# Casting the output by column halves, storing it from two engines, and a shorter last piece of the output projection

## The chip, the cores and the metric

One core of a Trainium2 chip. The metric is the device time of one execution, in microseconds (us). The median before the change is 525.68 us over the first 3 runs. The device time is some 2 us longer than the span of the trace, which runs from the first to the last instruction; positions below are in the span. In the views of the profile, PE is TensorE (the matrix products), DVE is VectorE, ACT is ScalarE and SP is SyncE; a q behind a name marks that engine's instruction queue, where stores are issued. The granted clock is the share of full speed that the chip allowed TensorE.

## The reference, cut to what matters

```
xn  = layernorm(x)                                   # x: [4, 1, 640]
out = x + attention(xn, k_cache, v_cache, wq, wo)    # 32 heads of 192, the last 2048 positions of the caches
        + (silu(xn @ w1) * (xn @ w3)) @ w2           # w1, w3: [640, 1536], w2: [1536, 640]
```

The last step of the attention is a product with wo ([6144, 640]). Its sum over the heads, the feed-forward part and x are added in one tile of PSUM (the memory that matrix products are summed in), which is cast to bf16 and stored: 4 rows of 640 values, 5 KB.

## The kernel before

Only the end of the program matters here. The sum `acc` is one tile of PSUM. This text and the recorded ones call the place of such a tile a bank, and the records call its two groups of rows, partitions 0 to 3 and 32 to 35, quadrants. `acc` holds columns 0 to 319 of the output on partitions 0 to 3, columns 320 to 639 on partitions 32 to 35. Every row of wo is so two matmuls. The last group of heads takes wo in three pieces, loaded last in the stream.

```python
CT, B, N0, RPP = 32, 4, 320, 12
acc = ps_acc.tile([P, N0], FP32, name="acc")
nc.vector.memset(acc[:], 0.0)
...
def acc_half(i, lhsT, rhs, first=False, last=False):
    nc.tensor.matmul(acc[i * CT:i * CT + B, :], lhsT=lhsT, rhs=rhs[:, i * N0:(i + 1) * N0], start=first, stop=last)
...
def ge_proj(hg, i0, i1, last=False):          # two matmuls for each row i of wo
    oT, wo_t = oTs[hg], wos[hg]
    for i in range(i0, i1):
        acc_add(oT[:, i, 0:B], wo_t[:, i * D:(i + 1) * D], last=last and i == RPP - 1)
...
WOC = [0, RPP - 5, RPP - 2, RPP]              # pieces of 7, 3 and 2 rows a partition
for h in range(H - 2, H):
    add(NU - 6, 0, load_v, h)
add(NU - 6, 0, w2_load)
for i0, i1 in zip(WOC, WOC[1:]):
    add(NU - 6, 0, wo_load, NG - 1, i0, i1)
    add(e, 6, ge_proj, NG - 1, i0, i1, True)
add(e - 1, 8, ffn_out)
...
res = ppool.tile([B, 2, N0], BF16, tag="pr", name="res")
nc.scalar.copy(out=res[:, 1, :], in_=acc[CT:CT + B, :])
nc.vector.tensor_copy(out=res[:, 0, :], in_=acc[0:B, :])
nc.scalar.dma_start(out=out.rearrange("b s d -> (b s) d"), in_=res[:].rearrange("b i n -> b (i n)"))
```

Of the kernel before, what the change touches and what calls it, by code (L numbers as in the profile page):

```python
# [11 lines left out]
BF16 = mybir.dt.bfloat16  # L12
# [52 lines left out]
def kernel(  # L65
# [20 lines left out]
    nc = tc.nc  # L86
    P = 128
    B, Sq, D = A_x.shape
# [13 lines left out]
    CT = 32  # L102
    HB = HG * CT // P
    QW = HG * Dh
    RPP = QW // P
    RW = Dh // RPP
    NU = H * GQ
    N0 = D // 2
# [17 lines left out]
    ppool = ctx.enter_context(tc.tile_pool(name="pr", bufs=PBUFS))  # L126
# [36 lines left out]
    for k0 in range(0, KC, 2):  # L163
        n = min(2, KC - k0)
        wt = vpool.tile([P, 2, H * Dh], BF16, tag="vt")
        nc.sync.dma_start(out=wt[:, 0:n, :].rearrange("p k n -> p (k n)"),
                          in_=wq_v[:, k0:k0 + n, :].rearrange("p k n -> p (k n)"))
# [26 lines left out]
    acc = ps_acc.tile([P, N0], FP32, name="acc")  # L194
# [39 lines left out]
    for i in range(2):  # L234
# [4 lines left out]
                          in_=xn[:, LB:LB + LS * LP].rearrange("b (i e s) -> b s e i", e=LE, s=LS))  # L239
# [246 lines left out]
    def add(slot, phase, fn, *args):  # L486
        sched[slot].append((phase, len(sched[slot]), fn, args))
# [45 lines left out]
    add(17, 6, x_add, 1)  # L533


    WOC = [0, RPP - 5, RPP - 2, RPP]
    for h in range(H - 2, H):
        add(NU - 6, 0, load_v, h)
    add(NU - 6, 0, w2_load)
    for i0, i1 in zip(WOC, WOC[1:]):  # L540
        add(NU - 6, 0, wo_load, NG - 1, i0, i1)
# [4 lines left out]
        for phase, _, fn, args in sorted(sched[s], key=lambda e: (e[0], e[1])):  # L546
            fn(*args)

    res = ppool.tile([B, 2, N0], BF16, tag="pr", name="res")
    nc.scalar.copy(out=res[:, 1, :], in_=acc[CT:CT + B, :])  # L550
    nc.vector.tensor_copy(out=res[:, 0, :], in_=acc[0:B, :])
    nc.scalar.dma_start(out=out.rearrange("b s d -> (b s) d"), in_=res[:].rearrange("b i n -> b (i n)"))


# [28 lines left out]
```

## Time and profile before

| | before |
|---|---|
| device time, median of the first 3 runs | 525.68 us (525.5 to 525.7) |
| span of the profiled run | 523.48 us |
| bytes read | 222.96 MB, 426 GB/s over the span |
| last completion of a piece of wo | 520.415 us |
| from there to the end of the program | 3.064 us |

The last row is what the change can reach. I call it **the tail**: from the moment when the last piece of wo is complete to the end of the span. It is measured in one profile with a resolution of some ns, while device times of the same kernel differ by up to 0.74 us from run to run. The lines of the page and of the timeline that show this are in the prediction below. One more view, the stretches (length, busy time of each engine with its number of instructions, granted clock, share of the DMA engines' time and GB/s), shows the DMA engines running dry while PE still works:

```profile
518.00:519.00 1.00, 0.45 (x8) 0.31 (x9) 0.00 (x0) 0.00 (x0) 0.00 (x0) 1.00 0.74 303
519.00:520.00 1.00, 0.98 (x16) 0.53 (x13) 0.00 (x0) 0.00 (x0) 0.00 (x0) 1.00 0.66 247
520.00:521.00 1.00, 0.69 (x8) 0.12 (x4) 0.07 (x1) 0.04 (x1) 0.00 (x0) 1.00 0.01 3
521.00:522.00 1.00, 0.00 (x0) 0.00 (x0) 0.41 (x1) 0.38 (x1) 0.00 (x0) 1.00 0.00 0
```

The DMA share goes from 0.66 to 0.01 at 520; after that come a few matmuls, two casts and a store, one behind the other.

### The profile page before, as it was taken

The numbers are of one execution on the slowest core, as the hardware profiler recorded it, in microseconds if no ns is written. First come the engines' busy times: TensorE is split into PE (matmuls) and PEld (weight loads), VectorE is DVE, ScalarE is ACT, GpSimd is POOL, SyncE is SP. The second block draws the span as 40 slices with busy tenths as digits, with TensorE's granted clock in tenths as the row PEclk, the third lists the DMA queues.
The fourth block names the chain that finished last, engine by engine and source line by source line (L and its number), as shares of the span: only waits on it lengthen the run. The fifth ranks groups of instructions, "written<-read, shape, count | busy, mean of one in ns | idle before, by whom it ended". The sixth has DMA issues, their size and how long they took to land.

```text
span 523.5 us, 4807 instructions
## 1 busy us (share of the span) xinstructions
PE 349.5 (67%) x2346; PEld 74.9 (14%) x1652; DVE 340.5 (65%) x397; ACT 57.3 (11%) x179; POOL 8.2 (2%) x11
## 2 busy tenths in 40 slices
PE   0695767784855787563767667763768677575785
PEld 0100111110111111010111111110111121111122
DVE  3369665485766767764667876673777767666861
ACT  2031111100101101110110111000011101011020
POOL 3200000000000000000000000000000000000000
PEclk9999877987899889987898998899788989899899
DMA  9999999999999999999999999999999999999996
GB/s 389 423 439 419 440 431 427 432 432 436 428 433 432 431 434 429 429 433 435 428 434 431 428 439 426 431 434 432 436 428 433 429 436 431 430 432 429 438 426 275
DMA packets 11155, 223.27 MB, mean 427 GB/s; under 512 B 1246, under 2 KB 1394, under 8 KB 1650
## 3 DMA queue, kind: packets, MB, share of 16 engines
q1 hardware_dynamic: 11118, 222.96, 99.2%
q8 instruction: 16, 0.26, 0.2%
q14 instruction: 5, 0.04, 0.0%
q10 hardware_dynamic: 16, 0.01, 0.0%
HBM read 222.96 MB, written 0.01 MB: 426 GB/s over the span
## 4 chain that ended last, share of the span: by engine, by line
DMA 61%; DVE 19%; PE 17%; ACT 2%; issue 1%; SPq 0%
DMA kt<-in_A_k_cache_dram 52%; DVE pr L301 12%; PE ps L312 8%; DMA wo_t<-in_A_wo_dram 7%; PE po L385 3%; PE qps L266 3%; DVE sc L320 3%; DMA x_sb<-in_A_x_dram 1%; DVE z L356 1%; ACT ex L348 1%; DVE xn L215 1%; PE mt L342 1%; PE f_ps L431 1%; ACT negm L345 0%; PE mt L329 0%
## 5 line engine op out<-in xcount | busy, mean ns | idle before, releaser
L312 PE MATMUL ps<-pr,idb 128*128 128x512 bf16 x768 | 207.2, 410 | 148.7 <-DVE pr L301 148.7
L301 DVE TENSOR_TENSOR pr<-kt,qbc 128x3072 bf16<-128x3072 bf16 x128 | 223.6, 1747 | 103.5 <-DMA kt<-in_A_k_cache_dram 103.5
L320 DVE TENSOR_REDUCE sc<-ps 128x16 f32<-128x512 f32 x128 | 87.1, 681 | 5.2 <-PE ps L312 5.2
L364 PE MATMUL o_ps<-vt,z 128*8 128x384 bf16 x1024 | 51.7, 342 | 0.9 <-DMA vt<-in_A_v_cache_dram 0.9
L385 PE MATMUL po<-o_sb,sel_w 128*32 128x192 f32 x128 | 48.5, 513 | 1.1 <-ACT o_sb L367 1.1
L364 PEld LDWEIGHTS <-z 128*8 128x8 bf16 x1024 | 24.0, 89 | 93.3 <-issue 82.1
L356 DVE TENSOR_TENSOR z<-ex,mask_b 128x256 bf16<-128x256 bf16 x32 | 13.6, 425 | 35.6 <-ACT ex L348 35.4
L367 ACT COPY o_sb<-o_ps 128x384 f32<-128x384 f32 x32 | 15.3, 478 | 181.0 <-PE o_ps L364 181.0
L337 ACT ACTIVATE gneg<-gmax 1x128 f32<-1x128 f32 x32 | 9.8, 308 | 173.9 <-DVE gmax L334 173.9
L329 PEld LDWEIGHTS mt<-idf,lmax 128*1 128x1 f32 x32 | 3.3, 104 | 143.8 <-issue 143.8
L385 PEld LDWEIGHTS po<-o_sb,sel_w 128*32 128x32 f32 x128 | 14.3, 131 | 28.1 <-issue 24.5
L312 PEld LDWEIGHTS <-idb 128*128 128x128 bf16 x123 | 11.8, 96 | 32.8 <-issue 31.7
L342 PEld LDWEIGHTS mt<-ones_ff,gneg 1*128 1x128 f32 x64 | 9.4, 182 | 47.2 <-issue 40.0
L266 PE MATMUL qps<-wt,xnT 128*128 128x512 bf16 x59 | 15.9, 433 | 0.1
L334 DVE TENSOR_REDUCE gmax<-mt 1x4 f32<-1x128 f32 x32 | 8.8, 275 | 6.9 <-PE mt L329 6.8
L345 ACT COPY negm<-mt 128x1 f32<-128x1 f32 x32 | 5.1, 159 | 70.0 <-PE mt L342 70.0
L342 PE MATMUL mt<-ones_ff,gneg 1*128 1x1 f32 x64 | 12.1, 256 | 0.7 <-ACT gneg L337 0.7
L372 PEld LDWEIGHTS po<-rsum,tot_w 128*32 128x32 f32 x64 | 4.5, 108 | 49.9 <-ACT ex L348 36.5
L220 PE MATMUL xnT_ps<-idb,xn 4*128 4x4 bf16 x5 | 0.4, 178 | 16.6 <-DVE xn L215 16.6
L348 ACT ACTIVATE ex<-sc,negm 128x64 bf16<-128x64 f32 x32 | 11.1, 347 | 1.0
L329 PE MATMUL mt<-idf,lmax 128*1 128x128 f32 x32 | 11.1, 346 | 0.0
L287 PE MATMUL acc<-wo_t,oT 128*4 128x320 bf16 x96 | 10.0, 318 | 1.1 <-DMA wo_t<-in_A_wo_dram 1.1
(74 smaller groups left out, 81.0 us busy)
## 6 DMA issues: line engine op xcount, KB each, us to landing
kt<-in_A_k_cache_dram SPq DMA_DIRECT2D x32, 3072.0 KB, 19.0
vt<-in_A_v_cache_dram SPq DMA_DIRECT2D x32, 3072.0 KB, 25.5
wt<-in_A_wq_dram SPq DMA_DIRECT2D x2, 3072.0 KB, 10.0
wo_t<-in_A_wo_dram SPq DMA_DIRECT2D x3, 1920.0 KB, 22.7
w<-in_B_w_dram SPq DMA_DIRECT2D x2, 1920.0 KB, 25.8
wt<-in_A_wq_dram SPq DMA_DIRECT2D x1, 1536.0 KB, 19.7
w<-in_B_w_dram SPq DMA_DIRECT2D x1, 1536.0 KB, 15.4
wo_t<-in_A_wo_dram SPq DMA_DIRECT2D x1, 1120.0 KB
```

The lines of the kernel that those rows point to most:

```text
L266: nc.tensor.matmul(qp[:], lhsT=xnT[:, kc].rearrange("p a b -> p (a b)"), rhs=wq_rows[kc][:, (c0 + i) * QC:(c0 + i + 1) * QC], start=(kc == ...
L287: nc.tensor.matmul(acc[i * CT:i * CT + B, :], lhsT=lhsT, rhs=rhs[:, i * N0:(i + 1) * N0], start=first, stop=last)
L301: nc.vector.tensor_tensor(out=pr[:], in0=kts[h][:, g * JQ:(g + 1) * JQ, :], in1=qbc[:, h * Dh:(h + 1) * Dh].unsqueeze(1).to_broadcast([P, ...
L312: nc.tensor.matmul(ps[:], lhsT=idb[:], rhs=pr[:, :, kk * DD:(kk + 1) * DD], start=(kk == 0), stop=(kk == NK - 1))
L320: nc.vector.tensor_reduce(out=scs[h][:, g * JQ:(g + 1) * JQ], in_=pss.pop(u)[:], axis=AX.X, op=ALU.add)
L329: nc.tensor.transpose(out=mt[0:1, 0:P], in_=chs[h][0][:], identity=idf[:])
L342: nc.tensor.matmul(mt[:, P:P + 1], lhsT=gneg[:].rearrange("o p b -> o (p b)"), rhs=ones_ff[:], start=True, stop=True)
L348: nc.scalar.activation(out=ex[:], in_=scs.pop(h)[:], func=ACTF.Exp, bias=negm[:, 0:1], scale=SCALE, accum_out=rsum[:])
L356: nc.vector.tensor_tensor(out=z[:], in0=ex[:].unsqueeze(2).to_broadcast([P, NJ, B]), in1=mask_b[:].unsqueeze(1).to_broadcast([P, NJ, B]), ...
L364: nc.tensor.matmul(o_ps[c * CT:c * CT + 2 * B, :], lhsT=z[:, 2 * jj:2 * jj + 2, :], rhs=vt[:, 2 * jj:2 * jj + 2, :], start=(jj < 4), stop= ...
L367: nc.scalar.copy(out=o_sb[:], in_=o_ps[:])
L385: nc.tensor.matmul(po_v[blk * CT:(blk + 1) * CT, :, x, :], lhsT=sel_w[:, par].rearrange("p a b -> p (a b)"), rhs=o_sb[:, par * Dh:(par + 1 ...
```

## The change

The intent: each cast works on 160 columns instead of 320, the output goes out in two smaller stores from two engines at once, and less is left to multiply when the last piece of wo arrives.

```diff
-    WOC = [0, RPP - 5, RPP - 2, RPP]
+    WOC = [0, RPP - 5, RPP - 1, RPP]
...
-    res = ppool.tile([B, 2, N0], BF16, tag="pr", name="res")
-    nc.scalar.copy(out=res[:, 1, :], in_=acc[CT:CT + B, :])
-    nc.vector.tensor_copy(out=res[:, 0, :], in_=acc[0:B, :])
-    nc.scalar.dma_start(out=out.rearrange("b s d -> (b s) d"), in_=res[:].rearrange("b i n -> b (i n)"))
+    res = ppool.tile([CT + B, N0], BF16, tag="pr", name="res")
+    nc.scalar.copy(out=res[:, N0 // 2:], in_=acc[0:CT + B, N0 // 2:])
+    nc.vector.tensor_copy(out=res[:, 0:N0 // 2], in_=acc[0:CT + B, 0:N0 // 2])
+    out_v = out.rearrange("b s d -> (b s) d")
+    nc.sync.dma_start(out=out_v[:, 0:N0], in_=res[0:B, :])
+    nc.scalar.dma_start(out=out_v[:, N0:], in_=res[CT:CT + B, :])
```

Both casts now read partitions 0 to 35 of the one bank, and each store needs both casts.

## The prediction

The lengths come from the trace of the kernel before, but the +0.05 for the stores is the author's estimate between 0 and 0.2. That the casts would be put in series was, apart from the split by row groups in the kernel before, a rule that no trace had shown; take the 6 to 4, and with it the mean of +0.05, as the author's guess. That 36 partitions take no longer than 4 was not shown before the run either. And the range was made wider than the spread of the three runs for a shift between chips; the medians of the kernel before on the three chips of the experiments were later 525.60, 525.68 and 525.61 us.

> **What bounds the kernel now.** I read the page first: the slices and the DMA queues.
>
> ```profile
> DMA  9999999999999999999999999999999999999996
> q1 hardware_dynamic: 11118, 222.96, 99.2%
> HBM read 222.96 MB, written 0.01 MB: 426 GB/s over the span
> ```
>
> The 16 DMA engines are nine tenths busy or more in 39 of 40 slices; only the last slice, 13 us wide, falls to 6. The kernel is a stream of 222.96 MB of caches and weights, read once. The change does not touch how many bytes are read, so it can act only after the stream runs dry. Its two parts, the cut of the last load of wo and the output, both lie there. So the second view is the timeline of the last 5 us (columns: start us, length us, engine, line, operation, shapes, count, idle before and what ended it):
>
> ```profile
> 518.55 1.71 PE L287 MATMUL acc<-wo_t,oT 128*4 128x320 bf16 x20 [0.87 <-DMA wo_t<-in_A_wo_dram]
> ...
> 520.46 0.44 PE L287 MATMUL acc<-wo_t,oT 128*4 128x320 bf16 x4 [0.20 <-DMA wo_t<-in_A_wo_dram]
> ...
> 520.93 0.48 DVE L551 CAST res<-acc 4x320 bf16<-4x320 f32 x1 [4.89 <-PE acc L287]
> 520.96 0.42 ACT L550 CAST res<-acc 4x320 bf16<-4x320 f32 x1 [7.69 <-PE acc L287]
> 521.48 0.27 ACTq L552 DMA_DIRECT2D out_dram<-res  x1
> ```
>
> To be seen: the last piece of wo releases four matmuls, they release two casts side by side, the casts release one store. The chain of waits confirms that nothing else is in it:
>
> ```profile
> 483.33 37.08 DMA wo_t<-in_A_wo_dram
> 520.41 0.04 issue
> 520.46 0.48 PE acc L287 x4
> 520.94 0.47 DVE res L551
> ```
>
> The rest of the span, to 523.48, is the store and the end of the program. The single records of the trace give the seams: the second last piece of wo is complete at 519.638 and the last at 520.415; the store's issue runs 521.481 to 521.752; its four packets of 1280 B start at 522.237 to 522.382 and take 58 to 68 ns; its last completion comes at 522.767. SyncE waits for it, runs two more waits, and the program closes 0.71 us later. From last byte to end: 523.48 - 520.42 = 3.06 us, 0.6% of the time. All that this change can move lies in those 3.06 us.
>
> [...]the casts overlap from 520.96 to 521.38 on one bank, DVE on partitions 0 to 3 and ACT on 32 to 35. [...]both casts now read partitions 0 to 35 of that bank. [...]the trace has 479, and its slope between the casts of 320 and 512 elements is (685-479)/192 = 1.07 ns an element[...]. [...]The trace's one store takes 0.27 us to issue and another second to land, for 5 KB: bytes are not what it costs.
>
> **The change part by part.** (1) wo in 7, 4, 1 rows of 1280 B a partition instead of 7, 3, 2. Each of 16 engines handles 8 packets a piece. A packet takes 102 ns at 2560 B and 149 at 3840; the line through 102 and 338 (8960 B) gives 196 at 5120 B, and 1280 B took 58 in the store. Per engine, 8 x (149+102) = 2008 ns becomes 8 x (196+58) = 2032: the last byte comes at the same time to some 0.02 us. But the middle piece is bigger and completes 8 x (196-149) = 0.38 us later, at about 520.0 instead of 519.64.
> Matmuls run in pairs (one for each half of the columns), a pair each 135 ns. Before: six in the middle piece from 519.68, done in 0.4 us, a gap of 0.20, then two pairs at 520.457 and 520.592. After: four pairs from about 520.03 (0.04 after the completion), at 520.03, 520.16, 520.30, 520.43; the fifth pair, of the last piece, could start at 520.46 by its data but comes in line at 520.57. The last pair thus starts at 520.57 instead of 520.59: **-0.02 us**, not the 0.135 that a pair less behind the last byte promises. The wait has moved to the middle piece. Given the unsure packet times, -0.03 to +0.03.
>
> (2) Each cast is 160 columns over 36 partitions instead of 320 over 4. [...]DVE: 479 - 160 x 1.07 = 308 ns. ACT: the slope of its casts is (607-416)/192 = 0.995, so 416 - 159 = 257 ns. Side by side, the later end comes at 479 - 308 = **-0.17 us**. In series, ACT first as the program has it: ACT starts 0.034 after DVE started, 257 ns, a hop of some 0.03 (a DVE instruction follows an ACT one at 508.04 to 508.07), then DVE 308: 0.63 us instead of 0.479, **+0.15 us**.
>
> (3) One store of 4 rows of 1280 B becomes two of 4 rows of 640 B. They need both casts each, and are issued side by side, on SyncE and ScalarE. The issue is on the path as before (0.27 us; on SyncE 0.38 to 0.64 for its big loads, so for 4 rows I take 0.27 too). Packets start 0.76 us after the issue begins, one each 50 ns; if the eight packets queue behind one another it costs four more, 0.2 us; if each issuer has its own path, nothing. I put in **+0.05**. SyncE, which sat in its closing waits, has to store first and then run six or so waits at 0.06 us each, 0.4 us, inside the second in which the store lands: 0 on the path, give or take 0.06 for the order of the last waits.
>
> Sum: with the casts in series -0.02+0.15+0.05 = **+0.18**; side by side -0.02-0.17+0.05 = **-0.14**.
>
> **The rivals.** *The casts overlap and the tail is 0.3 to 0.4 us shorter*, as the author means it: a pair of matmuls less, shorter casts, smaller stores. For it: the casts' slopes are real. Against: [...]the pair has nowhere to go. It makes 525.3. *The casts are put in series*: for it, [...]that the before kernel splits them by quadrants; against, no trace here shows an ordered read against a read. It makes 525.85. *Two stores are dearer than one*: each completes on its own and SyncE, busy with a store, reaches its closing waits late; against, 1 us of slack. It adds 0.2 to 0.4, to 526.1. *The small packets of the last piece cost bandwidth*: 128 packets of 1280 B; even at double their 58 ns it is 8 x 58 = 0.46 us on an engine, and the measured packets speak for 0.02.[...]
>
> **Range and chances.** I hold the series likelier, 6 to 4: 0.6 x 0.18 - 0.4 x 0.14 = +0.05, so 525.68 + 0.05 = 525.73, say 525.7. The branches reach from -0.4 to +0.5. The three runs before lie within 0.2 us[...]. So 525.1 to 526.3. Two per cent are 10.5 us, three times the entire tail; no part reaches that. Faster 0.005, same 0.985, slower 0.01[...].
>
> **What would show it.** Right: a timeline in which the two casts of 36x160 take about 0.31 (DVE) and 0.26 (ACT), with DVE waiting for ACT (series) rather than both for PE (overlap); the middle piece of wo releasing 8 matmuls near 520.0 and the idle time before the last two gone; the last byte of wo within 0.1 us of 520.4 from the start; two issues near 521.5, their packets near 522.3, one landing near 522.8. Wrong: last bytes that come over 0.3 us apart from before (then the stream moved, not the tail); casts that keep 0.4 us in spite of half the columns; a SyncE issue of 0.5 us, or a wait of SyncE that ends after the store has landed; a landing over 0.3 us later.

## The result, and the profile after

The changed kernel took 525.96 us (median of 6 runs, 525.65 to 526.03), the kernel before in the same rounds 525.65 (6 runs, 525.50 to 525.77). The ratio is 1.0005, 95% interval 0.9992 to 1.0018: the same. (A ratio is the mean time of one kernel's fast runs over that of the other's of the same rounds, so not quite the ratio of the medians.) The times alone do not show that the 0.31 us between the medians is real; the tail does. The timeline of the changed kernel's end:

```profile
518.53 1.11 PE L287 MATMUL acc<-wo_t,oT 128*4 128x320 bf16 x14 [0.88 <-DMA wo_t<-in_A_wo_dram]
...
520.04 0.84 PE L287 MATMUL acc<-wo_t,oT 128*4 128x320 bf16 x10 [0.39 <-DMA wo_t<-in_A_wo_dram]
...
520.92 0.28 ACT L550 CAST res<-acc 36x160 bf16<-36x160 f32 x1 [6.42 <-PE acc L287]
521.24 0.32 DVE L551 CAST res<-acc 36x160 bf16<-36x160 f32 x1 [3.97 <-ACT res L550]
521.58 0.31 SPq L553 DMA_DIRECT2D out_dram<-res  x1
521.59 0.28 ACTq L554 DMA_DIRECT2D out_dram<-res  x1
```

Two things differ from before. The 24 matmuls of wo stand in two groups, 14 and 10, not 14, 6 and 4: the last pair does not wait for its own piece any more. And the DVE cast names ACT's cast as what ended its idle time, where before it named PE: the casts are in series. The chain that ended last says the same; it has one engine more than before:

```profile
520.04 0.86 PE acc L287 x10
520.90 0.02 issue
520.92 0.29 ACT res L550
521.22 0.02 issue
521.24 0.32 DVE res L551
```

The tail, cut at the seams that the single records of the trace give (completions come from the updates of semaphores, the counters by which engines and transfers report that they are done; "the store" is always the one that lands last):

| us | before | changed | difference |
|---|---|---|---|
| a: last piece of wo complete to first cast | 0.511 | 0.520 | +0.009 |
| b: start of the first cast to end of the last | 0.479 | 0.634 | +0.155 |
| c: end of the casts to issue of the store | 0.076 | 0.028 | -0.048 |
| d: issue of the store to its last completion | 1.286 | 1.455 | +0.169 |
| e: last completion to end of the program | 0.712 | 0.712 | 0 |
| tail | 3.064 | 3.349 | +0.285 |

The last piece of wo completed at 520.400 instead of 520.415, so the span grew by 0.285 - 0.015 = 0.270 us, from 523.479 to 523.749. The whole effect is in this table, half in b, half in c and d.

### The profile page after: what moved, and what is told of

It is laid out like the page before. It is cut to its first block, busy times and chain, and to the rows that moved or that the text cites. A ratio compares the mean times of both kernels' runs of the same rounds, so it can differ in the third digit from the quotient of the medians.

```text
span 523.7 us, 4810 instructions
## 1 busy us (share of the span) xinstructions
PE 356.1 (68%) x2347; PEld 75.9 (14%) x1652; DVE 340.4 (65%) x397; ACT 57.2 (11%) x179; POOL 8.2 (2%) x11
## 4 chain that ended last, share of the span: by engine, by line
DMA 59%; PE 20%; DVE 16%; ACT 2%; issue 1%; SPq 0%
DMA kt<-in_A_k_cache_dram 52%; DVE pr L301 11%; PE ps L312 10%; DMA wo_t<-in_A_wo_dram 7%; PE po L385 4%; PE qps L266 3%; DVE sc L320 2%; ACT ex L348 1%; DVE z L356 1%; DMA x_sb<-in_A_x_dram 1%; DVE xn L215 1%; PE mt L342 1%; PE acc L287 1%; PE f_ps L431 1%; PE o_ps L364 1%
## 5 line engine op out<-in xcount | busy, mean ns | idle before, releaser
L312 PE MATMUL ps<-pr,idb 128*128 128x512 bf16 x768 | 209.7, 414 | 142.4 <-DVE pr L301 142.4
L364 PE MATMUL o_ps<-vt,z 128*8 128x384 bf16 x1024 | 56.8, 367 | 1.7 <-DMA vt<-in_A_v_cache_dram 1.7
L364 PEld LDWEIGHTS <-z 128*8 128x8 bf16 x1024 | 25.1, 93 | 100.1 <-issue 90.5
```

Of the source, the lines that this page charges most:

```text
L312: nc.tensor.matmul(ps[:], lhsT=idb[:], rhs=pr[:, :, kk * DD:(kk + 1) * DD], start=(kk == 0), stop=(kk == NK - 1))
L364: nc.tensor.matmul(o_ps[c * CT:c * CT + 2 * B, :], lhsT=z[:, 2 * jj:2 * jj + 2, :], rhs=vt[:, 2 * jj:2 * jj + 2, :], start=(jj < 4), stop= ...
```

## The experiments

Ten runs gave a result (nine new kernels and one repeat), all timed in five rounds beside the kernel before. No time differs from before clearly: every interval of a ratio includes 1 and reaches about 0.13% to either side, 0.7 us, so I read the tails. The three batches ran on three different chips.

| kernel | median, us | before in the same rounds | a | b | c | d | e | tail |
|---|---|---|---|---|---|---|---|---|
| before (first profile) | 525.68 | | 0.511 | 0.479 | 0.076 | 1.286 | 0.712 | 3.064 |
| changed (first profile) | 525.96 | 525.65 | 0.520 | 0.634 | 0.028 | 1.455 | 0.712 | 3.349 |
| cut_only | 525.71 | 525.60 | 0.508 | 0.479 | 0.076 | 1.296 | 0.717 | 3.076 |
| after_old_cut | 525.90 | 525.60 | 0.519 | 0.633 | 0.028 | 1.456 | 0.712 | 3.348 |
| after_quadrant_casts | 525.78 | 525.60 | 0.524 | 0.479 | 0.028 | 1.347 | 0.783 | 3.161 |
| after_two_banks | 525.80 | 525.60 | 0.529 | 0.316 | 0.063 | 1.467 | 0.779 | 3.154 |
| before_sp_store | 525.45 | 525.68 | 0.510 | 0.479 | 0.064 | 1.301 | 0.717 | 3.071 |
| after_both_act | 525.92 | 525.68 | 0.535 | 0.635 | 0.336 | 1.234 | 0.713 | 3.453 |
| after_dve_first | 525.98 | 525.68 | 0.513 | 0.638 | 0.025 | 1.445 | 0.717 | 3.338 |
| after_one_store | 525.47 | 525.61 | 0.514 | 0.636 | 0.027 | 1.215 | 0.648 | 3.040 |
| before_two_row_stores | 525.81 | 525.61 | 0.511 | 0.480 | 0.063 | 1.358 | 0.784 | 3.196 |
| after_again | 526.05 | 525.61 | 0.586 | 0.635 | 0.027 | 1.457 | 0.717 | 3.422 |

Theory at the start: the cut is worth nothing, the loss is the series of the casts, and the rest is something about SyncE's store. The rival: one of the three parts makes all of it.

### The cut of wo: cut_only and after_old_cut

cut_only is the kernel before with the new cut:

```diff
-    WOC = [0, RPP - 5, RPP - 2, RPP]
+    WOC = [0, RPP - 5, RPP - 1, RPP]
```

> Kernel before, with only the cut of wo changed (7, 4, 1 rows instead of 7, 3, 2). Call the tail the time from the last completion of wo to the end of the program: 3.06 us before, 3.35 us in the changed kernel. My theory (the cut is worth nothing, the matmuls queue behind the middle piece): middle piece completes near 520.0, releases 8 matmuls in a row with the last 2, no idle time before the last pair, tail 3.06 +- 0.05, time that of before within 0.15 us. Rival (a pair of matmuls less behind the last byte): tail 2.93. Rival (packets of 1280 B cost bandwidth): last completion 0.2 to 0.4 us later than 520.4, tail 2.9 to 3.1.

```profile
520.29 0.84 PE L287 MATMUL acc<-wo_t,oT 128*4 128x320 bf16 x10 [0.39 <-DMA wo_t<-in_A_wo_dram]
521.17 0.48 DVE L551 CAST res<-acc 4x320 bf16<-4x320 f32 x1 [4.90 <-PE acc L287]
```

The timeline of this run has ten matmuls in a row, as in the changed kernel. The middle piece completed at 520.252 and the last at 520.662, 0.41 us later; four pairs of matmuls at 0.135 us take 0.54, so the fifth pair, whose data were there, stood in line. Part a is 0.508 against 0.511, and the tail of 3.076 us is within the 3.06 +- 0.05. The rival that saves 0.13 falls. The last completion came 0.25 us later than in the first profile of before, which is what the rival of slow small packets had named. But over all profiles the new cut completed anywhere from 520.393 to 520.662 (eight profiles, mean 520.51) and the old one from 520.415 to 520.509 (four, mean 520.46): the end of the stream moves by as much among kernels with the same new cut, and a shift of 0.05 us between the cuts is neither shown nor excluded. One packet of 1280 B took 55 ns against 102 for 2560 B and 196 for 5120 B, so the small ones were not dear (128 packets of each size, in the first profiles of before and of the changed kernel).

after_old_cut is the changed kernel with the line reversed.

> Changed kernel with the old cut (7, 3, 2 rows). My theory: casts still in series (ACT 0.28, then DVE 0.32), two stores, tail 3.35 +- 0.05, time 0.2 to 0.4 us over before. Rival (the cut saves 0.13 us of matmuls in the changed kernel): tail 3.48. If the cut was what cost the 0.3 us: tail 3.06.

The tail is 3.348 us against 3.349. Counted from the last byte, the cut is worth nothing in either surroundings.

### The series of the casts: after_quadrant_casts, after_two_banks and after_dve_first

after_quadrant_casts keeps the cut and the two stores, and casts by row groups as before:

```diff
-    nc.scalar.copy(out=res[:, N0 // 2:], in_=acc[0:CT + B, N0 // 2:])
-    nc.vector.tensor_copy(out=res[:, 0:N0 // 2], in_=acc[0:CT + B, 0:N0 // 2])
+    nc.scalar.copy(out=res[CT:CT + B, :], in_=acc[CT:CT + B, :])
+    nc.vector.tensor_copy(out=res[0:B, :], in_=acc[0:B, :])
```

> Changed kernel (new cut, two stores), but the casts by row groups as before: DVE partitions 0 to 3, ACT partitions 32 to 35, 320 columns each, each store behind its own cast. My theory: the casts overlap again, later end 0.48 after their start instead of 0.63, so tail 3.35 - 0.155 = 3.20, the rest above 3.06 being the store of SyncE that lands late; 3.15 to 3.25. Rival (the two stores are the whole loss): tail 3.35. Rival (the series is the whole loss): tail 3.06 or less.

```profile
521.02 0.48 DVE L551 CAST res<-acc 4x320 bf16<-4x320 f32 x1 [4.92 <-PE acc L287]
521.06 0.42 ACT L550 CAST res<-acc 4x320 bf16<-4x320 f32 x1 [7.72 <-PE acc L287]
521.50 0.28 ACTq L554 DMA_DIRECT2D out_dram<-res  x1
521.53 0.31 SPq L553 DMA_DIRECT2D out_dram<-res  x1
```

In its timeline both casts name PE again and overlap; b is back at 0.479 and the tail at 3.161, inside the 3.15 to 3.25. Neither rival fits: the series is not the whole loss, nor are the stores. Each store now waits for one cast only, and ScalarE's goes out as its own cast ends, 0.028 us before SyncE's. SyncE's store still takes 1.347, less than the 1.455 of the changed kernel but 0.061 more than the one store before, and e is longer by 0.071; so the total of the expectation came out, while what stands above 3.06 is made up otherwise than it said.

after_two_banks puts columns 160 to 319 of both halves of the sum into a second PSUM bank (idle from the middle of the program on), so that each cast can read 36 x 160 of its own bank:

```diff
-        nc.tensor.matmul(acc[i * CT:i * CT + B, :], lhsT=lhsT, rhs=rhs[:, i * N0:(i + 1) * N0], start=first, stop=last)
+        for k, t in enumerate((acc, acc2[0])):
+            nc.tensor.matmul(t[i * CT:i * CT + B, 0:N0 // 2], lhsT=lhsT,
+                             rhs=rhs[:, i * N0 + k * (N0 // 2):i * N0 + (k + 1) * (N0 // 2)], start=first, stop=last)
...
-    nc.scalar.copy(out=res[:, N0 // 2:], in_=acc[0:CT + B, N0 // 2:])
+    nc.scalar.copy(out=res[:, N0 // 2:], in_=acc2[0][0:CT + B, 0:N0 // 2])
```

(acc2 is zeroed before x is added to it, and the adding of x is moved behind that; both lie mid-program.) The question is whether DVE still waits for ACT when the casts read the same partitions of two banks.

> Changed kernel, but the sum lies in two PSUM banks: columns 0 to 159 of both halves in the old one, 160 to 319 in a bank that is idle by then; each projection row becomes four matmuls of 160 columns instead of two of 320. Each cast reads 36 x 160 of its own bank. My theory[...]: DVE waits for PE and not for ACT, both casts start together, 0.28 and 0.32 us, tail 3.35 - 0.317 = 3.03, or 3.0 to 3.15 when four matmuls take a little longer than two. Rival (the casts of 36 partitions are ordered for another reason, or slow each other): DVE still waits for ACT or takes over 0.4 us, tail 3.3 or more.

```profile
520.22 0.86 PE L295 MATMUL acc<-wo_t,oT 128*4 128x160 bf16 x20 [0.37 <-DMA wo_t<-in_A_wo_dram]
521.12 0.32 DVE L561 CAST res<-acc 36x160 bf16<-36x160 f32 x1 [4.91 <-PE acc L295]
521.14 0.28 ACT L560 CAST res<-acc 36x160 bf16<-36x160 f32 x1 [7.70 <-PE acc L295]
```

DVE no longer waits for ACT. The casts of 36 x 160 run side by side at their lengths of the series, so it is neither their shape nor their 36 partitions that ordered them, and 20 matmuls of 160 columns take 0.86 us where 10 of 320 took 0.84. Part b falls to 0.316, by 0.318 as expected. This is what the change was after. The tail of 3.154 still lies above the 3.03 that I had put first, and just outside the 3.0 to 3.15: with two casts to wait for, c goes back to 0.063, and e is 0.067 longer (below). The second bank is also a second tile, so this run does not tell apart an order made for the place in PSUM and one made for the tile as such; that casts of disjoint row groups of one tile are not ordered, the kernel before shows (they start at 520.926 and 520.960).

after_dve_first swaps the two cast lines of the changed kernel.

> Changed kernel with the two cast lines in the other order. If the order of the series is that of the program: ACT waits for DVE, 0.32 then 0.28 us with the same hop, later end 0.63 after the first start as before, tail 3.35 +- 0.06. If the chip and not the program orders them: DVE and ACT in the same order as in the changed kernel, or both at once.

```profile
521.08 0.32 DVE L550 CAST res<-acc 36x160 bf16<-36x160 f32 x1 [4.84 <-PE acc L287]
521.43 0.29 ACT L551 CAST res<-acc 36x160 bf16<-36x160 f32 x1 [7.96 <-DVE res L550]
```

The order turns with the program: now ACT waits for DVE. The series is a semaphore in the compiled program: in the trace of the changed kernel DVE's cast waits for semaphore 104, which ACT's cast raises at 521.215, and starts at 521.237; in the kernel before both casts wait for 105, the matmuls' own.

### The stores: before_sp_store, after_both_act, after_one_store and before_two_row_stores

In the changed kernel SyncE's store lands 1.455 us after its issue began, ScalarE's 1.271. before_sp_store is the kernel before with its one store on SyncE. The rival below is that SyncE's store is slow only beside another.

```diff
-    nc.scalar.dma_start(out=out.rearrange("b s d -> (b s) d"), ...
+    nc.sync.dma_start(out=out.rearrange("b s d -> (b s) d"), ...
```

> Kernel before, its one store issued by SyncE instead of ScalarE. In the changed kernel the store of SyncE landed 1.46 us after its issue began, that of ScalarE 1.27 us (1.29 in the kernel before). Theory (SyncE's store is slower by itself): 1.45 from issue to landing, tail 3.06 + 0.15 = 3.2. Rival[...]: 1.3, tail 3.06 +- 0.06.

It took 1.301 us, against 1.286 from ScalarE. My theory that SyncE's store is slower by itself falls. Its median of 525.45 is the lowest of the correct kernels, but the ratio is 1.0000 (0.9986 to 1.0013) and its tail that of before.

after_both_act issues both stores from ScalarE:

```diff
-    nc.sync.dma_start(out=out_v[:, 0:N0], in_=res[0:B, :])
+    nc.scalar.dma_start(out=out_v[:, 0:N0], in_=res[0:B, :])
```

> Changed kernel, both stores issued by ScalarE one after the other. Theory (SyncE's store is slower by itself): the second store is issued some 0.3 us later and lands 1.27 after its issue begins: tail 3.35 + 0.3 - 0.18 = 3.47. Rival (two stores in flight delay each other): 3.6 or more, or the second lands over 1.4 us after its issue.

```profile
521.60 0.26 ACTq L553 DMA_DIRECT2D out_dram<-res  x1
521.90 0.31 ACTq L554 DMA_DIRECT2D out_dram<-res  x1
```

The number of the theory came out (3.453 against 3.47), but for the other reason. Issued 0.30 us apart, the packets of the second store start 0.24 us after the last packet of the first (522.685 and 522.448), and the stores land 1.186 and 1.234 us after their issues: apart, neither is slow. The rival's number was for stores in flight together, which these are not.

after_one_store leaves out ScalarE's store (half of the output is never written, a wrong result):

```diff
-    nc.scalar.dma_start(out=out_v[:, N0:], in_=res[CT:CT + B, :])
```

> Changed kernel without the store of ScalarE (half of the output is never written: a wrong result on purpose). Open: why the store of SyncE lands 1.46 us after its issue begins beside another store, and one alone in 1.29 to 1.30. Theory (company: two stores in flight at once[...] delay the completions of the later one): alone the same store of 4 rows of 640 B lands after 1.27 to 1.32, tail 3.35 - 0.16 = 3.19. Rival (rows of 640 B with gaps between them are slow by themselves when SyncE writes them): 1.45, tail 3.35.

The same store of SyncE, alone, lands in 1.215 us: 0.240 less than beside the other one, and less than the 1.27 to 1.32 of my theory (the tail is 3.040, not 3.19; 0.064 of this is part e). Of this, 0.095 is in the packets: the last completion packet (4 B; one follows each row) starts 0.878 us after the issue began, against 0.973 with the eight data packets of both stores interleaved. The other 0.145 lies between that packet and its semaphore update, 0.337 us alone and 0.482 in company. In the changed kernel all of SyncE's four completions (522.885 to 523.037) come after all of ScalarE's (522.708 to 522.857), though its packets had started before the last of the other's. Why the completions line up like this the trace does not show.

before_two_row_stores splits the one store of the kernel before by rows: rows 0 and 1 from SyncE, rows 2 and 3 from ScalarE, whole rows of 1280 B.

```diff
-    nc.scalar.dma_start(out=out.rearrange("b s d -> (b s) d"), in_=res[:].rearrange("b i n -> b (i n)"))
+    nc.sync.dma_start(out=out_v[0:B // 2, :], in_=res[0:B // 2].rearrange("b i n -> b (i n)"))
+    nc.scalar.dma_start(out=out_v[B // 2:, :], in_=res[B // 2:].rearrange("b i n -> b (i n)"))
```

> Kernel before, its store split in two by rows: rows 0 and 1 from SyncE, rows 2 and 3 from ScalarE, 2 packets of 1280 B each, at the same moment. Theory (company of two stores): the later one lands 0.1 to 0.2 us later than a store alone (1.29), that is 1.4 or more, tail 3.15 to 3.25. Rival (the two stores of the changed kernel write halves of the same rows of the output, and that is what delays them): both land within 1.25 to 1.32, tail 3.06 +- 0.05.

ScalarE's landed in 1.171 us and SyncE's in 1.358: a miss for both numbers, between 1.32 and 1.4. The later of two stores is again behind, by 0.19 us to its companion and 0.07 to the one whole store, so sharing rows of the output is not needed for it. The tail grew to 3.196, with the casts and the cut as before. Two stores in place of one cost 0.13 here, 0.06 of it in c and d and 0.07 in e. In every run with two stores in flight at once the one behind is SyncE's, whose packets also start later; whether it trails because it is second or because it is SyncE's in company, no run tells apart.

### How well a tail repeats: after_again

> The changed kernel once more, unchanged, to see how well a tail repeats. Both theories: tail 3.35 +- 0.03, the store of SyncE landing 1.44 to 1.47 after its issue began, time 0.2 to 0.4 us over before. If the tail comes out over 0.1 us apart from 3.35, the single profiles of the other runs do not carry what was read from them.

Parts b, c, d and e repeat to 0.005 us; a does not: 0.586 against 0.520, tail 3.422, past the 0.03 that I allowed though under 0.1. The timeline and the stretches of this run say why:

```profile
518.98 2.15 PE L287 MATMUL acc<-wo_t,oT 128*4 128x320 bf16 x24
```

```profile
517.00:518.00 1.00, 1.00 (x12) 0.49 (x8) 0.00 (x0) 0.00 (x0) 0.00 (x0) 0.50 0.84 347
518.00:519.00 1.00, 1.00 (x12) 0.48 (x10) 0.00 (x0) 0.00 (x0) 0.00 (x0) 0.50 0.69 287
519.00:520.00 1.00, 1.00 (x12) 0.58 (x10) 0.00 (x0) 0.00 (x0) 0.00 (x0) 0.65 0.67 244
520.00:521.00 1.00, 1.00 (x18) 0.57 (x12) 0.00 (x0) 0.00 (x0) 0.00 (x0) 1.00 0.05 18
```

The granted clock (the third number from the right) was 0.50 from 516.29 to 519.70, so PE came late to its backlog: all 24 matmuls stand in one row without a wait for any piece, and the last pair started 0.241 us after the last piece was complete, 0.176 in the first profile. Where such a stretch falls differs from profile to profile: 510.63 to 514.05 in the first one of the changed kernel, before the last pieces, but 516.05 to 519.46 in after_quadrant_casts and 515.58 to 519.00 in after_both_act, where a is 0.524 and 0.535. Part a is therefore known to some 0.07 us; b to e are not touched by it.

### Not settled: the closing waits

Part e takes few values, and they go with the number of closing waits that SyncE runs after the one that the last store ends: 0.648 with one (after_one_store), 0.712 with two (before, changed), 0.784 with three (before_two_row_stores), 0.06 to 0.07 us each. It goes with the place of the store's semaphore in SyncE's list, and not with its number alone: semaphore 102 has two waits behind it in the changed kernel and three in after_quadrant_casts. A kernel made to put that wait last (before_wait_last: the store of before on SyncE, and an early load cut in seven to shift the semaphores; 0.58 us expected, an estimate: 0.648 less one wait) found no chip; this stays a reading of the profiles, and with it a tail of 2.94 (estimated as 3.07 - 0.13), which would have been the best, is untried. None of the correct kernels that ran has a tail under that of before.

## Why the prediction was right, by its own steps

**The bound and the reach.** Right: the stream carries the time, the change acts in the last 3.06 us, and the tail is now 3.35. The range of 525.1 to 526.3 held 525.96, but it would have held the other branch too (525.68 - 0.14 = 525.54), and 525.7 was a mean of both branches: it is the trace and not the time that tells which came true. Two readings of the prediction are off, and nothing rests on them: the "second" in which the store lands is a microsecond (522.767 - 521.752 = 1.015 us), and SyncE's loads take 0.33 to 0.95 us to issue over the whole trace, not 0.38 to 0.64.

**The cut, -0.02 us.** Right: +0.009 in part a, -0.003 in cut_only. The middle piece completed at 519.995 (predicted 520.0), the pair started in line at 520.576 (predicted 520.57), the packet of 5120 B took 196 ns (predicted 196). The smaller last piece made the piece ahead of it later (519.995 against 519.638), and the work waited there.

**The casts, +0.15 us in series.** Right, and the branch was chosen right, though on a rule that no trace had shown: +0.155. The sum was better than its terms. DVE took 317 ns (predicted 308), ACT 285 (predicted 257), but ACT also started right after the matmuls and not 0.034 us behind. 36 partitions of 160 columns took less than 4 of 320 on both engines (317 against 479 ns, 285 against 416), so it is the columns that counted. The slope of 0.995 ns a column for ACT was mis-sized: it came from casts of 512 columns that ran in another stage. (416-285)/160 = 0.82 is what the two shapes at the end of the program give. after_quadrant_casts takes the 0.155 back, after_dve_first turns the order round, after_two_banks removes it.

**The stores, +0.05 us.** The step that was mis-sized: c and d together made +0.121, and that is why the sum of +0.18 fell short of +0.285. The two effects that I weighed, eight packets in line and the issue, are the smaller part: 0.095 us of packets. What I did not weigh is the 0.145 us by which the completions of SyncE's store trail. Against these stand 0.071 us by which a store of 2.5 KB alone is faster than the one of 5 KB (1.215 and 1.286), and 0.048 us saved ahead of the issue, because in series the one wait on the last cast covers both casts (both stores wait for semaphore 101 alone, which DVE's cast raised at 521.565): 0.095 + 0.145 - 0.071 - 0.048 = 0.121. One landing near 522.8 was foretold; the one that counts came at 523.037. SyncE's closing waits were no danger, as predicted: it stood at the decisive one from 522.07, a us ahead of the landing.

**The rivals.** The casts side by side: not in this kernel, and true as soon as the two halves lie in two banks, though even then the tail was 3.154 and not 0.3 to 0.4 us shorter. Two casts at once on the same partitions of one bank did not occur: in every run with such a pair the second waited for the first (it started 0.032 us after the other's end in the changed kernel), and every kernel that stored all of its output gave correct results. What a pair at once would do, no run shows. Two stores dearer than one: partly true, by 0.12 us in c and d and not 0.2 to 0.4, and not by the late SyncE that it named. Small packets: 55 ns, no loss seen.

## What to carry to other kernels

When both engines read one tile of PSUM, look in the trace whether one waits for the other. Here halves of the columns made two casts of 0.28 and 0.32 us in series, where a split by row groups let casts of 0.42 and 0.48 overlap, and a bank for each half let the short casts run side by side (521.12 and 521.14 in after_two_banks). A shorter last load helped nothing, since the work of the load ahead of it was not done by then (four pairs of matmuls took 0.54 us, the last piece came 0.41 behind, in cut_only); count the matmuls that stand in line. For the 5 KB of output here a second store saved nothing and landed later than one alone, and at such sizes the thing to read is the tail in the trace, since 0.3 us in 526 is below what the times can show.
